# Transposing all of x beside the second stage of a convolution, and giving the dense slices to the third

## The chip, the cores and the metric

The kernel runs on one core of one Trainium2 chip. The metric is the time of one execution on the device in microseconds (us); lower is better. Six runs of the kernel before took 2141.81 to 2153.86 us, with a median of 2148.28.

## The reference

Two unrelated computations share one launch; their outputs stand side by side.

*A* is a long convolution over a sequence of 2048 rows and 1024 channels. A key is filtered with four taps, multiplied by a value, convolved along the sequence with a kernel `ssm_k` as long as the sequence, and multiplied by a query:

```python
y_f = rfft(kv_pad) * rfft(ssm_k_pad)
y = irfft(y_f)[:S] + kv * ssm_D
out_a = q * y
```

*B* is a recurrent attention over 64 segments of 32 rows. Each segment sees its own rows and an 8-row memory, and its output at the memory's rows is the memory of the next segment:

```python
for s in range(64):
    h = concat([mem, x[32*s:32*s+32]])
    q, k, v = h @ Wq, h @ Wk, h @ Wv          # 1024 -> 32 heads x 128
    o = softmax(mask(q @ k.T * scale)) @ v
    o = o @ Wo
    mem, out_b[s] = o[:8], o[8:]
```

All inputs and outputs are bf16.

## The kernel before, in words

**A in three stages.** The transforms are done as matrix products with sines (a transform of 4096 as 128 times 32). Stage 1 makes the first half of the transform of u (the product of filtered key and value) and of the convolution kernel, and stores both to scratch tensors in HBM, SU and SK. Stage 2 has 17 sets of frequencies, each in two halves of 512 channels: 34 *units*. A unit (`unit_front`, `unit_back`) takes the gathered tiles Kg and Ug, multiplies them by tables on TensorE (Kre, Kim, Ure, Uim into PSUM, line 323), copies Kre and Kim to SBUF on ScalarE (L335, L336), forms the complex product on VectorE (pa, pb, pc, pd, L343 to L346, and Yim, L350) and GpSimd (Yre, L349), and multiplies back into z on TensorE (L358, L360), which ScalarE copies to zs (L362) and stores to the scratch SZ (L301). The matmuls of a unit fill half of TensorE's columns (L323) or of its rows (L358, L360), and two of them run side by side. Stage 3 has 16 rows of work: each loads a tile zt from SZ (L389) and every second one a tile qt (L396), both on SyncE's queue; TensorE makes y from zt with four matmuls (L392), VectorE multiplies it by qt into ot (L399), and GpSimd's queue stores ot for two rows at once (L401).

**B's preparation beside it.** Before the recurrence starts, the parts of B that do not depend on the memory are computed by plain dense products, for the memory-sized part of each segment. XBT, the transposed rows of x that the dense products use, is made between stages 1 and 2. `dense` (from L608) is a generator that gives one *slice* at a time: eight matmuls of 128x512 (L614) into a PSUM tile kb_ps, then a copy to a tile `stage` by `evac` (two of three on ScalarE, L603, one on VectorE, L605). Sixteen slices make one group. The first group (K, first half) runs between stages 1 and 2. Three more groups, 48 slices, are given by `slices`: K's second half, Q's first half, Q's second half. When a group is finished, its result is stored to a scratch tensor REC in four stores (L643), one for each later call of `fill`. The weights of these groups lie in tiles Wmid and pw. Two of the pw tiles for Q's second half (pw 2 and 3) can be loaded (L567) only when the group before, which uses the tiles, is through.

The recurrence also needs all of x transposed, not only the memory-sized part. `x_block(b)` (from L584) takes one of 16 blocks of 128 rows: eight TensorE transposes (L591) from X_sb into a PSUM tile xt_ps, one copy to xt (L593), one 256 KB store to REC on GpSimd's queue (L594). X_sb is one buffer that holds two blocks; `x_load` (L580) loads it on SyncE's queue, right after the second block of the pair before has been transposed. xt is one buffer for two blocks as well, so the first copy of a pair waits until both stores of the pair before have landed. xt_ps and kb_ps share a pool of two PSUM buffers.

**What sets the order.** `fill` is called after each of the 34 units of stage 2 and after each of the 16 rows of stage 3; n counts the calls, 0 to 49. In the kernel before, n with n % 3 == 2 gives a block of x, so that 11 blocks (n = 2, 5, ..., 32) lie in stage 2 and 5 in stage 3. Every other unit of stage 2 gives one dense slice (23), and every row of stage 3 gives one slice as well (16). Nine slices are left and follow stage 3; then comes the projection V (L749), 256 matmuls of the same size, for which the weights Wres and Wmore are loaded (L563, L567) into memory that stage 3 held until its last y. At odd n above 5 a weight tile is copied to the scratch WS (L669), from n = 29 on six chunks of Wo are copied to WS (L663). A scheduler then orders the instructions of each engine by its own estimates of their times: it moves the matmuls of a slice between those of neighbouring units, and some past the end of a stage. Each engine and each DMA queue then works through its own list in that fixed order.

**The recurrence.** 64 steps of attention with weights streamed from WS (L709); its order is written out by hand, and the change does not touch it.

Of the kernel before, what the change touches and what calls it, by code (L numbers as in the profile page):

```python
# [405 lines left out]
def b_kernel(ctx: ExitStack, tc, x, mem0, Wq, Wk, Wv, Wo, outb, n_seg, run_a):  # L406
    nc = tc.nc
# [35 lines left out]
    def dram_chunk(ch):  # L443
        m, a, g = ch
        return Wo_v[a] if m == 3 else W_v[m][a, g]

    def dst_view(ap, ch):
        return ap.rearrange("p (hh d) -> p hh d", hh=2) if ch[0] == 3 else ap

    def stream_src(ch):  # L450
        return WS[ring_order.index(ch), :, 0:2048]
# [123 lines left out]
    copies = []  # L575
    loaded = {}

    def x_load(b):
        t = base.tile([128, 2048], BF, tag="wring2", name="X_sb")
        x_loads.append(nc.sync.dma_start(t[:].rearrange("p (b d) -> p b d", b=2),  # L580
                                         x[b * 128:(b + 2) * 128, :].rearrange("(b p) d -> p b d", b=2)))
        loaded[b], loaded[b + 1] = t[:, 0:1024], t[:, 1024:2048]

    def x_block(b):  # L584
        X_sb = loaded.pop(b)
        if b % 2 == 0:
            t = base.tile([128, 2048], BF, tag="wring3", name="xt")
            xts[b], xts[b + 1] = t[:, 0:1024], t[:, 1024:2048]
        tp = ps0.tile([128, 1024], BF, tag="ps0", name="xt_ps")
        for kc in range(8):  # L590
            nc.tensor.transpose(tp[:, kc * 128:(kc + 1) * 128], X_sb[:, kc * 128:(kc + 1) * 128], ident[:])  # L591
        xt = xts.pop(b).rearrange("p (s k t) -> p s k t", s=4, k=8)
        nc.vector.tensor_copy(xt, tp[:].rearrange("p (k j t) -> p j k t", k=8, j=4))  # L593
        rec_stores.append(nc.gpsimd.dma_start(REC[:, 4 * b:4 * b + 4, 0:256], xt.rearrange("p s k t -> p s (k t)")))  # L594

    xts = {}
# [44 lines left out]
    def store():  # L641
        if stores:
            nc.gpsimd.dma_start(*stores.pop(0))  # L643

    units = [0]
    blocks = list(range(n_seg // 4))
    wo_copies = [ch for ch in ring_order if ch[0] == 3]

    def q1_load(kc, k, ins):
        res[1, kc, 1] = pw(k)[:]  # L650
        with tc.issue_after(ins):
            group(1, 1, which=[kc], ws=q1, held=True)

    def fill(behind=None):
        store()
        n = units[0]
        units[0] += 1
        if n == 0:
            x_load(0)
        if n >= WO_COPY and wo_copies:  # L660
            ch = wo_copies.pop(0)
            with tc.issue_after(rec_stores[-1].ins):
                nc.gpsimd.dma_start(dst_view(stream_src(ch), ch), dram_chunk(ch))  # L663
        if n in Q_LOAD:
            i = Q_LOAD.index(n)
            q1_load(kept_q1[i][1], 4 + i, behind.ins)
        if n > 5 and n % 2 and copies:
            with tc.issue_after(rec_stores[-1].ins):
                copied.append(nc.gpsimd.dma_start(*copies.pop(0)))  # L669
        if n % 3 == 2 and blocks:  # L670
            b = blocks.pop(0)
            x_block(b)
            if b % 2 and blocks:
                x_load(b + 1)
        if n >= 34 or n % 3 != 2:
            next(rest, None)

    run_a(ps0, pw, slot16, stage1_done, fill)

    wres3 = ctx.enter_context(tc.tile_pool(name="b_wres", bufs=1, reuse_waits="tile"))  # L680
# [173 lines left out]
    with tc.manual_schedule():  # L854
# [53 lines left out]
        for s in range(n_seg):  # L908
            b, j = s // NB, s % NB
# [256 lines left out]
```

## Time and profile before

| | us |
|---|---|
| median of six runs | 2148.28 |
| the profiled execution, its own time | 2148.14 |
| span of its records, from first to last instruction | 2145.6 |
| stage 2, first to last matmul | 144.0 to 276.4 |
| first y of stage 3 to start of the last | 286.0 to 337.8 |
| dense slices left over | 338.6 to 355.5 |
| V projection | 355.5 to 411.8 |
| recurrence | 411.8 to 2145.6 |

How to read the profile: a table by windows gives, for each stretch of time, the microseconds for which each engine was busy and in brackets how many instructions it ran; then the TensorE clock that was granted as a share of full speed, the mean busy share of the 16 DMA engines, and what they moved. PE is the TensorE matmul, PEld its weight load, DVE is VectorE, ACT ScalarE, POOL GpSimd, SP SyncE. Matmuls overlap each other in the records, so the distance between their starts says more than their duration. A timeline row gives the start, the duration, the engine, the line, what is written and what it is made from, and in square brackets how long the engine was idle before it and what ended that. A name with a q behind it (SPq) is the engine's own queue of commands. A row of a group ends with total busy time and mean nanoseconds of one instruction, and after the second bar the idle time before them and what ended it.

Over the whole span TensorE is busy for 81%, the DMA engines move 374 GB/s on average, and the granted clock is 0.982.

### The profile page before, as it was taken

How to read it: one execution, taken by the hardware profiler on the slowest of the kernel's cores; microseconds unless marked ns; L12 is line 12 of the kernel's file. 1: busy time of each engine (PE TensorE's matmuls, PEld its weight loads, DVE VectorE, ACT ScalarE, POOL GpSimd, SP SyncE). 2: the span in 40 equal slices, each digit the busy share in tenths (PEclk: the TensorE clock that was granted, in tenths of full speed). 3: DMA queues.
4: the chain of work that ended last, by engine and by line, in shares of the span. 5: the costliest groups of instructions: out<-in, count | busy, mean ns of one | idle time of the engine just before them, and what ended most of it. 6: DMA issues, size and time to landing. Idle time of an engine off the chain costs nothing. (4 is left out here: it accounts for less than half of the span.)

```text
span 2145.6 us, 81545 instructions
## 1 busy us (share of the span) xinstructions
PE 1743.6 (81%) x35732; PEld 944.1 (44%) x35764; DVE 866.2 (40%) x2735; ACT 638.2 (30%) x1131; POOL 431.6 (20%) x1108
## 2 busy tenths in 40 slices
PE   6889879888888888788778877878877878887886
PEld 2433334344444444444444444444444444444444
DVE  9828842133333333333333333333333333333332
ACT  6946511222222222222222222222222222222221
POOL 3114522211111111111111111111111111111111
PEclk9999999999999999999999999999999999999999
DMA  8989899999999999999999999999999999999996
GB/s 306 364 322 355 297 342 381 309 396 385 382 388 393 390 392 391 390 387 392 382 385 393 393 389 379 391 390 384 374 385 378 390 388 389 393 396 390 377 383 268
DMA packets 238313, 802.29 MB, mean 374 GB/s; under 512 B 34722, under 2 KB 34754, under 8 KB 237956
## 3 DMA queue, kind: packets, MB, share of 16 engines
q1 hardware_dynamic: 206036, 724.01, 87.9%
q0 software_dynamic: 26704, 62.59, 8.5%
q10 hardware_dynamic: 5216, 10.49, 1.3%
q8 instruction: 279, 4.57, 0.9%
q14 instruction: 78, 0.64, 0.1%
HBM read 737.56 MB, written 62.39 MB: 373 GB/s over the span
## 5 line engine op out<-in xcount | busy, mean ns | idle before, releaser
L942 PEld LDWEIGHTS <-rec 128*32 128x32 bf16 x12351 | 322.7, 96 | 463.8 <-issue 239.6
L942 PE MATMUL acc<-wring,rec 128*32 128x512 bf16 x3765 | 377.6, 385 | 128.6 <-DMA wring<-WS 113.2
L951 ACT CAST qkv_sb<-acc 128x512 bf16<-128x512 f32 x384 | 225.1, 586 | 648.9 <-PE acc L942 646.0
L1028 PEld LDWEIGHTS <-OT 128*32 128x32 bf16 x8192 | 222.0, 98 | 182.0 <-issue 154.2
L1028 PE MATMUL yacc<-wring,OT 128*32 128x256 bf16 x3072 | 156.0, 280 | 98.0 <-DMA wring<-WS 62.1
L942 PE MATMUL acc<-Wmid,rec 128*32 128x512 bf16 x3072 | 227.1, 384 | 0.0
L942 PE MATMUL acc<-Wres,rec 128*32 128x512 bf16 x2816 | 221.6, 380 | 0.0
L888 PEld LDWEIGHTS <-OTB 128*16 128x16 bf16 x4096 | 105.4, 89 | 101.6 <-issue 93.0
L1014 ACT CAST OT<-OTp 128x512 bf16<-128x512 f32 x128 | 75.0, 586 | 243.6 <-PE OTp L1006 243.4
L1044 DVE COPY KT<-tps 128x512 bf16<-128x512 bf16 x64 | 27.2, 425 | 292.8 <-PE tps L957 292.8
L1015 DVE CAST OTB<-OTp 128x128 bf16<-128x128 f32 x128 | 37.4, 292 | 263.0 <-ACT OT L1014 263.0
L843 POOL DMA_DIRECT2D rec<-REC x64 | 37.5, 586 | 518.7 <-issue 264.0
L787 DVE TENSOR_SCALAR wring<-OTp 128x384 int32<-128x384 int32 x126 | 112.3, 891 | 53.5 <-PE acc L942 45.6
L942 PE MATMUL acc<-pw,rec 128*32 128x512 bf16 x1544 | 132.1, 385 | 0.0
L918 POOL COPY KT<-rec 128x128 bf16<-128x128 bf16 x128 | 38.9, 304 | 418.5 <-PE SB L966 410.7
L903 POOL DMA_DIRECT2D out_dram<-YB x128 | 73.3, 579 | 242.8 <-DVE YB L901 222.6
L972 DVE TENSOR_REDUCE mx<-SB 128x5 f32<-128x200 f32 x128 | 47.1, 368 | 177.1 <-PE SB L966 177.0
L888 PE MATMUL SB<-wring,OTB 128*16 128x256 bf16 x1488 | 78.7, 275 | 39.4 <-DVE SB L867 30.7
L957 PEld LDWEIGHTS <-qkv_sb 128*128 128x128 bf16 x1024 | 62.9, 97 | 105.7 <-ACT qkv_sb L951 68.4
L957 PE MATMUL tps<-ident,qkv_sb 128*128 128x128 bf16 x1024 | 101.4, 222 | 8.0 <-DVE wring L787 0.2
L1028 PE MATMUL yacc<-Wlate,OT 128*32 128x256 bf16 x2048 | 105.5, 276 | 1.3 <-ACT qkv_sb L951 0.7
L1084 ACT CAST Y<-yacc 128x256 bf16<-128x256 f32 x64 | 23.8, 373 | 249.7 <-PE yacc L1028 245.7
(233 smaller groups left out, 2692.7 us busy)
## 6 DMA issues: line engine op xcount, KB each, us to landing
wring<-WS SPq DMA_DIRECT2D x1215, 512.0 KB, 7.4
rec<-REC POOLq DMA_DIRECT2D x64, 192.0 KB, 6.1
SK<-s_sb SPq DMA_DIRECT2D x16, 512.0 KB, 7.0
SU<-s_sb SPq DMA_DIRECT2D x16, 512.0 KB, 8.2
Kg<-SK SPq DMA_DIRECT2D x32, 256.0 KB, 5.1
Ug<-SU SPq DMA_DIRECT2D x32, 256.0 KB, 6.6
REC<-stage POOLq DMA_DIRECT2D x16, 512.0 KB, 10.7
zt<-SZ SPq DMA_DIRECT2D x16, 512.0 KB, 8.2
```

The lines of the kernel that those rows point to most:

```text
L787: nc.vector.tensor_scalar(out=dst, in0=src, scalar1=0, scalar2=None, op0=ALU.bitwise_or)
L843: nc.gpsimd.dma_start(rec[:], REC[:, s, :])
L888: nc.tensor.matmul(self.acc[32 * dq:32 * dq + W, x - o:y - o], lhsT=self.OTB[:, c, 4 * g + i, :], rhs=r, start=first and not self.seeded, ...
L903: nc.gpsimd.dma_start(bass.AP(outb.tensor, outb.offset + (SEG * NB * self.b + NX) * 2048 + 256 * dq, [[2048 * SEG, NB], [2048, 8], [1, 256 ...
L918: nc.gpsimd.tensor_copy(KT[:, :, :, 32:40], KBs[:, 128 * g:128 * g + 128].rearrange("p (c i t) -> p i c t", c=4, i=4))
L942: nc.tensor.matmul(self.acc[32 * c:32 * c + 32, x - 512 * c:y - 512 * c], lhsT=hT[:, kc, :], rhs=r, start=(kc == 0 and x == 512 * c), stop ...
L951: nc.scalar.copy(sb[:], self.acc[:])
L957: nc.tensor.transpose(tp[:, i * 128:(i + 1) * 128], sb[:, i * 128:(i + 1) * 128], ident[:])
L972: nc.vector.tensor_reduce(out=mx[:], in_=S, op=ALU.max, axis=AX.X)
L1014: nc.scalar.copy(OT[:], o_view[:, :, :, 0:32])
L1015: nc.vector.tensor_copy(OTB[:, :, 4 * g:4 * g + 4, 8 * j:8 * j + 8], o_view[:, :, :, 32:40])
L1028: nc.tensor.matmul(yacc[32 * dq:32 * dq + 32, x - o:y - o], lhsT=OT[:, c, i, :], rhs=r, start=(h == 0 and x == o), stop=(h == 31), tile_po ...
```

## The change

All of x is transposed beside stage 2: a block at every odd n, so that blocks 0 to 15 come at n = 1, 3, ..., 31. The other units of stage 2 give one dense slice each (17). In stage 3 the calls give one slice at even n and two at odd n (24). By this count seven slices are left for after stage 3. The copy from xt_ps to xt moves from VectorE to ScalarE. The copies of weight tiles to WS move from odd to even n. Buffers, loads and stores are the same.

```diff
         xt = xts.pop(b).rearrange("p (s k t) -> p s k t", s=4, k=8)
-        nc.vector.tensor_copy(xt, tp[:].rearrange("p (k j t) -> p j k t", k=8, j=4))
+        nc.scalar.copy(xt, tp[:].rearrange("p (k j t) -> p j k t", k=8, j=4))
         rec_stores.append(nc.gpsimd.dma_start(REC[:, 4 * b:4 * b + 4, 0:256], xt.rearrange("p s k t -> p s (k t)")))
...
-        if n > 5 and n % 2 and copies:
+        if n > 5 and n % 2 == 0 and copies:
             with tc.issue_after(rec_stores[-1].ins):
                 copied.append(nc.gpsimd.dma_start(*copies.pop(0)))
-        if n % 3 == 2 and blocks:
+        if n % 2 and blocks:
             b = blocks.pop(0)
             x_block(b)
             if b % 2 and blocks:
                 x_load(b + 1)
-        if n >= 34 or n % 3 != 2:
+        for _ in range(1 + n % 2 if n >= 34 else 1 - n % 2):
             next(rest, None)
```

## The prediction

> **What bounds the kernel now.** I read the page's time slices first, then a table of windows by stage, then the timelines of TensorE, VectorE, SyncE and GpSimd over those windows, and last the waits of each line that the change touches.
>
> ```profile
> core 0: us, PE busy (x) PEld busy (x) DVE busy (x) ACT busy (x) POOL busy (x), PEclk, DMA share, GB/s
> 144.00:276.40 132.40, 122.51 (x676) 41.66 (x686) 108.36 (x190) 78.79 (x150) 66.92 (x67) 1.00 0.93 323
> 276.40:286.00 9.60, 6.66 (x35) 2.98 (x36) 1.72 (x3) 1.76 (x3) 1.58 (x2) 1.00 0.79 283
> 286.00:338.60 52.60, 39.07 (x171) 16.61 (x174) 22.56 (x22) 4.10 (x7) 13.11 (x16) 0.94 1.02 391
> 338.60:355.50 16.90, 16.79 (x78) 7.64 (x79) 4.26 (x8) 3.52 (x6) 1.84 (x3) 1.00 0.92 338
> 355.50:411.80 56.30, 55.10 (x252) 25.03 (x256) 6.92 (x10) 12.89 (x22) 17.64 (x21) 1.00 0.94 328
> 411.80:2145.60 1733.80, 1389.57 (x33985) 796.12 (x33983) 624.41 (x2244) 441.30 (x833) 304.16 (x958) 0.98 1.00 384
> ```
>
> The rows are stage 2, the gap to stage 3, stage 3, the dense slices left over, the V projection, and the recurrence. The change touches only the first four; the last two keep their instructions, so I carry 56.3 and 1733.8 us over unchanged. Stage 2 is TensorE's (122.5 of 132.4 us busy, and little of the rest is queued elsewhere); stage 3 is held by transfers (DMA share 1.02, TensorE 39 of 52.6); the dense rest and V are TensorE's again.
>
> Inside stage 2 the pace follows from the order of the built instructions on TensorE. From the timeline: a dense or y matmul takes a slot of 0.216 us, a pair of 64-row or 64-column ones 0.216 for both, a transpose 0.056, and each change between these shapes adds 0.11 (a lone pair starts 0.32 after the last). Counted so, the 70 us from unit 5 to unit 24 come out 3.6% short, so I scale counts by 1.036. Two stalls stand out of it:
>
> ```profile
> 230.88 0.23 PE L591 MATMUL xt_ps<-ident,X_sb 128*128 128x128 bf16 x1
> 231.14 0.38 SPq L580 DMA_DIRECT2D X_sb<-in_B_x_dram  x1
> ...
> 239.29 0.45 PEld L591 LDWEIGHTS <-X_sb 128*128 128x128 bf16 x8 [0.23 <-DMA X_sb<-in_B_x_dram]
> ...
> 245.42 0.69 DVE L593 COPY xt<-xt_ps 128x1024 bf16<-128x1024 bf16 x1 [6.50 <-DMA REC<-xt]
> ```
>
> X_sb is one buffer for two row blocks: the next load goes out 0.3 us after the second block's last transpose and here lands 8.1 us later, just when TensorE comes back, three units on. And the copy to xt, also one buffer per pair, waited 6.5 us on VectorE for the pair before to be stored. From unit 24's first matmul to unit 27's took 16.4 us where the count gives 11.3: that wait costs TensorE 5.1 us.
>
> **The change, part by part.**
>
> *Dense slices and blocks in stage 2.* By the code, stage 2 gets 17 slices in place of 23 and 16 blocks in place of 11. The built order says less: up to the last z matmul TensorE has 165 dense matmuls (194 before), 128 transposes (96) and 291 changes of shape (263). So -29 x 0.216 = -6.3, +32 x 0.056 = +1.8, +28 x 0.11 = +3.1: only -1.4 us. Of this, unit 4 must be left out: its Kg lands no earlier, at 158.9 us. From there the count is 107.3 before and 105.1 after: **-2.2 us**.
>
> *Moved transfers.* Each block brings half a 512 KB load on SP and a 256 KB store on POOL. Stage 2 moved 42.7 MB; four more blocks bring 2 MB, while K's stage stores (four of 512 KB) move from units 23-26 to its last units. 323 GB/s stands against 391 in stage 3, so I cost bandwidth at nothing; if that cover is missing, 2 MB at 391 GB/s cost 5 us. On SP, the next sets' gathers stand behind X_sb's issue, but a set is fetched some four units (14 us) ahead and lands within 5 to 7: nothing; without that lead each pair would lose about 1 us. On POOL four more store issues of 0.78 us, and the copies to WS at even instead of odd units, stand ahead of Yre; POOL is busy for 67 of 132 us and waits 49 us for pb: nothing, uncovered 3 us.
>
> *The X_sb load.* This is the wait that the change adds. Between a pair's last transpose and the next pair's first, TensorE now has, counted and scaled, 3.9, 5.6, 6.3, 6.3, 5.7, 6.3 and 6.3 us (before: 8 to 11). It needs 0.3 + landing. Landings of these loads in stage 2 were 6.5 to 8.1 us, median 7.2. So waits of 2.7 (the first gap holds unit 4's wait too), 1.9, 1.2, 1.2, 1.8, 1.2, 1.2: **+11.2 us**, all on TensorE, with z and the next unit's matmuls queued behind. Ends: at 5.6 us (the shortest landing) 1.6, at 8.1 us 17.5. The Trainium skill, "DMA: Bandwidth & Descriptors", Measured, gives 0.95 us for 64 KB and 6.15 for 1 MB, leaving out descriptor emission; between them 512 KB is an estimated 3.3 us, under every gap, and the waits would be 0. The row has the other queues' traffic in it, so I take the row.
>
> *The store wait.* The 5.1 us go, for the place of that collision goes: K's stage stores no longer lie between blocks 7 and 8. Also about **1** us of today's X_sb waits (weight loads, 1.6 us in three). But ScalarE now waits where VectorE did, with Kre, Kim and zs queued behind it. A store is issued some 1.35 us after its copy starts and landed after 4.9 to 10.1 us, median 6.4 in stage 2. With the X_sb wait the next pair's copy follows 8.3 to 10.1 us after: enough up to 6.9 us of landing. Ends: 0, and 7 x 1.3 = 9 us at 8.2, a stage-3 landing. Near the median: **+1**.
>
> *The copy on ScalarE.*
>
> ```profile
> L249 ACT COPY kt<-k_tp 128x1024 bf16<-128x1024 bf16 x16 | 16.4, 1053 | 3.4 <-PE k_tp L247 3.4
> L593 DVE COPY xt<-xt_ps 128x1024 bf16<-128x1024 bf16 x16 | 10.9, 683 | 14.6 <-DMA REC<-xt 14.4 <-PE xt_ps L591 0.2
> ```
>
> The first row is a ScalarE copy of the same size and memories: 1.05 us for VectorE's 0.68. ScalarE's two units hold four Kre/Kim at 0.48, four zs at 0.53, two thirds of a dense copy (0.4) and two store issues (0.82): 5.3 us, with xt 6.3. TensorE needs 7.0 for two units. Cost nothing; uncovered it would be 16 x 1.05 = 17 us. The Trainium skill, "ScalarE: Activation LUTs", Rules for kernel authors, speaks against it: simple work belongs on VectorE, up to 3x faster. At 3 x 0.68 = 2.05 us ScalarE would need 7.3 us and set the pace, +4 us in all. The row says 1.5x, so I keep nothing. VectorE's freed 0.68 per block gains nothing either: it had 18% slack.
>
> Stage 2: -2.2 - 5.1 - 1 + 11.2 + 1 = **+3.9 us**, ending near 280.
>
> *Stage 3.* The gap stays 9.6 us: it is the last SZ store's landing and the first zt load.
>
> ```profile
> 312.24 0.38 PE L614 MATMUL kb_ps<-XBT,pw 128*128 128x512 bf16 x1 [4.52 <-DVE xt L593]
> 312.49 0.76 POOL L594 DMA_DIRECT2D REC<-xt  x1 [4.56 <-DMA pw<-in_B_Wq_dram]
> ...
> 337.77 1.02 PE L392 MATMUL y_ps<-zt,G2h 128*128 128x512 bf16 x4 [1.63 <-DMA zt<-SZ]
> ```
>
> The 4.5 us at 312 are put down to xt, but the weights pw of Q's second half landed there too (issued 303.3, 8.9 us). They can be loaded only once the second dense group is through, which in the new order is just before y10, not after y7. So y0 to y10 takes its ten zt steps of 2.5 us (TensorE has 22.0 of it), pw is issued 0.5 us later and lands after 8.9: 34.9 us. Behind the waiting matmul then stand y12 to y15 and 54 dense matmuls, 11.7 + 2.6 us to y15's start: 49.2 against 51.7 before: **-2.5**. The zt loads of y13 to y15 queue on SP behind pw, but have 8 us to spare at 8 us of landing, none at the 16.9 seen. Four blocks' stores and copies leave the stage; they were hidden or in the stall. Ends: -6 (1.5 MB at 391 GB/s less, and pw at 6.5) to +5.
>
> *The dense rest.* It has 72 matmuls for 78, -1.3 us. But V's eighth weight chunk landed 18.5 us after y15's start, and TensorE would want it at 0.9 + 15.6 + 1.5 = 17.9: 0.6 us of it turns into a wait: **-0.7**. The -3.5 us that two slices fewer would suggest is not there.
>
> Sum: +3.9 - 2.5 - 0.7 = +0.7 on the profiled execution's own 2148.14 us (span 2145.6 and 2.5 outside), which is the median of 2148.28 within 0.15: **2149 us**.
>
> **Rivals.** *Slower: stores too late for ScalarE.* Its place is the first xt copy of each pair; it decides from a store landing of 6.9 us. For it: VectorE waited 14.4 us there with three units of room, and now there are two. Against: most landings of stage 2 were below. At 8.2 us for stores and 8.1 for X_sb: +9 - 1 + 6.3 = +14, so 2163; with half of that, 2156.
> *Faster: X_sb comes in time.* If the last waits vanish (landing 5.6 us, seen in stage 3), 11.2 becomes 1.6: 2139. For it: TensorE's waits also thin out the traffic. Against: no landing in stage 2 was so short.
> *Slower in stage 3:* pw and zt landing late (16.9 us), +5 instead of -2.5: 2157; part of the slower case.
>
> **Numbers.** A measurement of this kernel can tell about 0.3%, 6.4 us, from no change. Forecast (within that) 0.44; faster 0.27, around 2139 to 2141; slower 0.29, around 2156. The range 2139 to 2160 leaves out about 2 in 10.
>
> **What would show it.** Right: xt transposes waiting 1 to 2 us for X_sb once per pair; stage 2's last z near 280; no VectorE wait for REC; a pw wait of some 8 us near y11; y15 near 339; V at 356. Wrong: ScalarE waits for REC of more than 5 us in sum, landings of X_sb below 6 us, or a stage 2 under 128 us.

## The result, and the profile after

The changed kernel took 2155.54 us (median of 34 runs, 2144.30 to 2168.03), the kernel before on the same chips 2148.08 (71 runs, 2139.36 to 2163.67): a ratio of 1.003, 95% interval 1.0019 to 1.0040, so 4 to 9 us slower. The forecast of 2149 is 6.5 us too low; the range holds the time.

The profiled execution of the changed kernel has a span of 2147.1 us, near the low end of its runs. Its recurrence took 1726.6 us where that of before took 1733.8, though its instructions are the same. So the comparison is made up to V's end, and over all kernels: the median less the end of V in the one profile lies between 1732 and 1740 us for before, after and the twelve experiments alike. By and large the differences between the medians come from the first 420 us; but the 8 us between these figures are as large as the loss itself, so a single profile shows where a time goes and not how large it is in the median. Windows by stage, in the columns used before:

```profile
core 0: us, PE busy (x) PEld busy (x) DVE busy (x) ACT busy (x) POOL busy (x), PEclk, DMA share, GB/s
142.80:285.30 142.50, 125.65 (x678) 43.96 (x689) 102.94 (x177) 91.46 (x163) 70.31 (x72) 0.95 0.88 306
285.30:296.40 11.10, 6.67 (x31) 2.83 (x30) 0.69 (x1) 2.34 (x4) 0.17 (x1) 0.94 1.02 342
296.40:347.00 50.60, 43.41 (x179) 17.98 (x183) 21.46 (x20) 5.86 (x10) 10.83 (x13) 0.95 0.95 348
347.00:362.50 15.50, 15.45 (x73) 7.02 (x73) 4.27 (x8) 2.93 (x5) 1.85 (x3) 1.00 1.01 354
362.50:420.50 58.00, 55.58 (x254) 25.12 (x258) 7.36 (x12) 12.89 (x22) 18.25 (x25) 1.00 0.93 340
```

Read against the rows of before: stage 2 grew from 132.4 to 142.5 us, the gap from 9.6 to 11.1, V from 56.3 to 58.0; stage 3 and the dense rest shrank by about 2 and 1.3. In stage 2 TensorE is busy for 3 us more and idle for 7 us more, and its granted clock is 0.95, not 1.00. Where in stage 2 this happens shows in the start of each unit's first product (pa, VectorE), counted from the first Kre matmul; the last three rows are experiments, told below:

| us from first Kre | unit 4 | unit 6 | unit 21 | unit 33 | last z |
|---|---|---|---|---|---|
| before | 17.4 | 24.9 | 79.1 | 128.4 | 132.4 |
| after | 18.3 | 32.9 | 90.2 | 137.2 | 142.4 |
| first pair early | 18.7 | 27.3 | 84.4 | 130.1 | 135.8 |
| all halves, early, ScalarE | 19.1 | 28.5 | 87.6 | 133.0 | 138.7 |
| all halves, early, VectorE | 18.5 | 26.3 | 80.2 | 125.7 | 130.3 |

Seven of the ten microseconds are lost between units 4 and 6 (14.6 us against 7.5). From unit 6 to unit 33 the two kernels take the same (104.3 and 103.5), though before has its REC stall in there. At the loss, SyncE's queue and then TensorE in the changed kernel:

```profile
154.85 0.32 SPq L293 DMA_DIRECT2D Ug<-SU  x1
157.60 0.38 SPq L580 DMA_DIRECT2D X_sb<-in_B_x_dram  x1
158.35 0.79 SPq L293 DMA_DIRECT2D Kg<-SK  x1
```

```profile
153.77 0.62 PE L591 MATMUL xt_ps<-ident,X_sb 128*128 128x128 bf16 x8
...
160.47 0.64 PE L323 MATMUL Uim_ps<-Ug,Mim 128*64 128x512 bf16 x2
166.71 1.03 PE L591 MATMUL xt_ps<-ident,X_sb 128*128 128x128 bf16 x8 [5.60 <-DMA X_sb<-in_B_x_dram]
```

Block 1 is transposed by 154.4. The load of the next pair goes out at 157.60, not 0.3 us later: SyncE's queue waited 2.4 us before it, by the trace until a Ug gather had landed. It lands after 9.1 us, and TensorE has stood still for 5.6. Then the clock (rows of 3.41 us of the changed kernel, then two rows of 4 us of before):

```profile
155.19:158.60 3.41, 1.38 (x8) 0.50 (x5) 0.42 (x1) 1.09 (x3) 0.04 (x1) 1.00 1.05 389
158.60:162.01 3.41, 2.51 (x8) 0.41 (x7) 3.38 (x7) 3.35 (x6) 1.93 (x2) 0.50 1.05 344
162.01:165.43 3.42, 0.00 (x0) 0.00 (x0) 1.96 (x4) 0.00 (x0) 1.14 (x1) 0.50 1.01 362
165.43:168.84 3.41, 2.13 (x14) 1.09 (x16) 0.00 (x0) 0.10 (x1) 0.00 (x0) 0.50 0.15 58
168.84:172.25 3.41, 3.08 (x11) 0.93 (x8) 1.30 (x3) 2.05 (x4) 0.00 (x0) 0.50 0.56 171
172.25:175.66 3.41, 3.41 (x17) 1.00 (x16) 1.60 (x3) 2.49 (x5) 1.36 (x2) 1.00 0.79 295
```

```profile
156.00:160.00 4.00, 2.44 (x14) 0.81 (x12) 1.07 (x2) 1.74 (x4) 1.64 (x2) 1.00 1.04 370
164.00:168.00 4.00, 3.73 (x19) 1.15 (x18) 3.41 (x7) 2.82 (x7) 2.48 (x4) 1.00 1.04 378
```

The first figure after the five busy times is the clock: 0.50 from 158.6 to 172.25. It fell before the wait for X_sb began (161.1): TensorE had just stood for 2.0 us before unit 4's Kre, by the trace for the copy of the Kre before it, which ScalarE started only when a Kg gather had landed. So the wait for X_sb did not bring the clock down; it kept it down. From 166.7 to 172.3 TensorE works at half speed (starts 0.43 us apart, not 0.216), which costs an estimated 2.8 us, half of this stretch, beside the wait.

The end of stage 2 (TensorE's timeline, after):

```profile
280.57 0.38 PE L360 MATMUL z_ps<-Yim,Nim 64*128 64x512 bf16 x1
...
285.01 0.39 PE L358 MATMUL z_ps<-Yre,Nre 64*128 64x512 bf16 x1
285.23 0.38 PE L360 MATMUL z_ps<-Yim,Nim 64*128 64x512 bf16 x1
...
296.45 1.01 PE L392 MATMUL y_ps<-zt,G2h 128*128 128x512 bf16 x2 [4.48 <-DMA zt<-SZ]
```

The last z stands behind 4.1 us of dense matmuls in TensorE's fixed order, and y0 comes 11.2 us after it.

### The profile page after: what moved, and what is told of

Read it like the earlier page. It is cut to its first block, busy times and chain, and to the rows that moved or that the text cites. A ratio compares the mean times of both kernels' runs of the same rounds, so it can differ in the third digit from the quotient of the medians.

```text
span 2147.1 us, 81561 instructions
## 1 busy us (share of the span) xinstructions
PE 1743.4 (81%) x35732; PEld 940.6 (44%) x35764; DVE 858.3 (40%) x2719; ACT 652.8 (30%) x1147; POOL 431.4 (20%) x1108
## 5 line engine op out<-in xcount | busy, mean ns | idle before, releaser
L1028 PEld LDWEIGHTS <-OT 128*32 128x32 bf16 x8192 | 217.1, 96 | 176.9 <-issue 149.6
## 6 DMA issues: line engine op xcount, KB each, us to landing
REC<-stage POOLq DMA_DIRECT2D x16, 512.0 KB, 10.1
```

The source lines that it names most:

```text
L1028: nc.tensor.matmul(yacc[32 * dq:32 * dq + 32, x - o:y - o], lhsT=OT[:, c, i, :], rhs=r, start=(h == 0 and x == o), stop=(h == 31), tile_po ...
```

## The experiments

All were measured with the kernel before beside them; the table gives the profiled parts in us (from the first Kre matmul to the last z, to y0, to y15, to V, to V's end, and their sum). Each profile is one execution, and the part sums follow the ratios only by and large.

| kernel | stage 2 | gap | stage 3 | rest | V | sum | ratio to before, 95% |
|---|---|---|---|---|---|---|---|
| before | 132.4 | 9.7 | 51.7 | 17.7 | 56.5 | 268.0 | |
| after | 142.4 | 11.2 | 49.6 | 16.4 | 58.2 | 277.9 | 1.0030 (1.0019 to 1.0040) |
| after, copies on VectorE | 137.7 | 13.4 | 53.3 | 16.4 | 56.9 | 277.6 | 1.0066 (1.0043 to 1.0090) |
| before, copies on ScalarE | 140.5 | 7.2 | 54.4 | 19.4 | 57.0 | 278.5 | 1.0030 (1.0017 to 1.0043) |
| before, stage 3 changed | 133.8 | 10.4 | 54.6 | 11.2 | 71.9 | 281.9 | 1.0064 (1.0040 to 1.0087) |
| after, first pair early | 135.8 | 10.8 | 50.8 | 16.4 | 57.7 | 271.5 | 1.0012 (0.9998 to 1.0026) |
| after, half loads | 138.7 | 11.3 | 48.6 | 16.4 | 59.3 | 274.2 | 1.0007 (0.9991 to 1.0023) |
| after, z first | 139.5 | 14.1 | 54.8 | 16.4 | 56.3 | 281.2 | 1.0048 (1.0033 to 1.0063) |
| after, stage 3 undone | 144.1 | 11.1 | 44.8 | 32.5 | 55.4 | 288.0 | 1.0070 (1.0047 to 1.0093) |
| early, VectorE | 137.4 | 14.3 | 52.9 | 16.4 | 58.1 | 279.1 | 1.0039 (1.0024 to 1.0054) |
| before, all halves | 137.3 | 9.4 | 53.2 | 17.7 | 57.0 | 274.6 | 1.0021 (1.0003 to 1.0038) |
| all halves, early | 138.7 | 10.7 | 51.9 | 16.4 | 58.2 | 275.9 | 1.0004 (0.9988 to 1.0020) |
| all halves, early, VectorE | 130.3 | 13.6 | 53.7 | 16.4 | 57.7 | 271.8 | 1.0015 (0.9999 to 1.0031) |
| the same, K's stores held | 131.3 | 9.8 | 54.3 | 16.4 | 57.3 | 269.1 | 1.0012 (0.9999 to 1.0025) |

**The copies back on VectorE.**

```diff
-        nc.scalar.copy(xt, tp[:].rearrange("p (k j t) -> p j k t", k=8, j=4))
+        nc.vector.tensor_copy(xt, tp[:].rearrange("p (k j t) -> p j k t", k=8, j=4))
```

> The changed kernel with the xt copies back on VectorE, nothing else. Theory A (the lost time is TensorE's wait for X_sb at the second pair and the half clock behind it): the same as the changed kernel, 2153 to 2158 us, and the 5.6 us X_sb wait near 161 to 167 us of the profile stays. Theory B (the ScalarE copy stands ahead of Kre and Kim, and VectorE's products, Yre and z come late by it): VectorE's waits for Kre fall from 25.7 us to about 5, and the time falls by 4 to 8 us, to 2148 to 2151.

2160.2 us: neither theory, 3.6 in a thousand slower than after. VectorE's waits for Kre do fall (us in total, times, longest; after first, then here):

```profile
DVE pa L343 <- ACT Kre L335: 25.7, 16, 6.9
```

```profile
DVE pa L343 <- ACT Kre L335: 5.1, 3, 2.1
```

In the profile stage 2 is 4.8 us shorter, with a wait of 6.2 us for X_sb in it, and the gap and stage 3 are 5.8 us longer: what stage 2 gains here is given back behind it. The profiled execution took 2151.65 us and was the fastest of its nine; why the median is slower than after's, the profile does not show. The built order explains stage 2: up to the last z it has 241 changes of shape and 158 dense matmuls, after has 291 and 165, which at 0.11 and 0.216 us is 7.0 us less to do.

**The copies on ScalarE alone, on the kernel before.**

```diff
-        nc.vector.tensor_copy(xt, tp[:].rearrange("p (k j t) -> p j k t", k=8, j=4))
+        nc.scalar.copy(xt, tp[:].rearrange("p (k j t) -> p j k t", k=8, j=4))
```

> The kernel before with only the xt copies moved to ScalarE. Theory A and the prediction's term (a copy on ScalarE costs nothing): 2145 to 2150 us, no change against before. Theory B: 11 copies in stage 2 at the same price give two thirds of the loss, 2152 to 2155, with VectorE's waits for Kre above 15 us (4.8 before).

2156.2 us, 0.30% slower, and waits for Kre of 20.7 us: what theory B expected, 1 us above its range. Stage 2 is 8.1 us longer. Its order has 20 more dense matmuls and 11 more changes of shape before the last z (274 for 263), 5.5 us; the rest goes with a clock of 0.86 and 0.80 between 150 and 170 us. One line on another engine has reordered TensorE.

**Stage 3 alone, on the kernel before.**

```diff
-        if n >= 34 or n % 3 != 2:
+        for _ in range(1 + n % 2 if n >= 34 else n % 3 != 2):
             next(rest, None)
```

> The kernel before with only stage 3's slices changed: three for every two rows. The prediction's terms for stage 3 and the dense rest, taken for this kernel: -2.5 us there and less in the rest, 2144 to 2147 us. Rival C (the weights of Q's second half and the zt loads come late behind the denser work): 2150 to 2157.

2162.43 us, 0.64% slower, more than either side expected. Only one slice is left for the dense rest, and V starts 2.3 us earlier, before its weights (TensorE's waits in V):

```profile
PE vb_ps L749 <- DMA Wres<-in_B_Wv_dram: 11.6, 6, 4.7
PE vb_ps L749 <- DMA Wmore<-in_B_Wv_dram: 2.0, 2, 1.5
```

Rival C had a loss, but by other transfers. The part belongs to a kernel whose stage 2 gives fewer slices, as the later run with stage 3 undone shows.

**The first pair early.** Blocks 0 and 1 at units 0 and 1.

```diff
-        if n % 2 and blocks:
+        if (n == 0 or n % 2 and n != 3) and blocks:
             b = blocks.pop(0)
```

> The changed kernel with the first two row blocks at units 0 and 1 in place of 1 and 3, so that the second X_sb load goes out some 7 us earlier; the other blocks stay. Theory A: the X_sb wait of 5.6 us at the second pair and the half clock (0.50 from 160 to 172 us) go, and the time falls by 4 to 8 us, to 2148 to 2151. Theory B: within 2 us of the changed kernel, 2154 to 2158.

2152.34 us, between the two ranges; the ratio goes from 1.0030 to 1.0012. Units 4 to 6 take 8.6 us, not 14.6, and TensorE waits 1.2 us for X_sb in all. The clock still falls, with hardly a wait for X_sb, but for 6.8 us in place of 13.7:

```profile
159.19:162.60 3.41, 2.58 (x12) 0.91 (x12) 2.99 (x5) 3.41 (x8) 1.15 (x1) 0.50 1.05 370
162.60:166.02 3.42, 3.32 (x12) 0.74 (x12) 3.30 (x6) 1.85 (x3) 2.33 (x3) 0.50 1.03 343
166.02:169.43 3.41, 3.19 (x15) 0.96 (x15) 2.26 (x4) 2.23 (x5) 0.93 (x2) 1.00 1.04 403
```

Taken whole, the edit gives back 6.3 of the 9.8 us in the profiles and, with intervals that still overlap, about half of the loss in the medians. Not all of it is the wait of theory A: the built order has 21 fewer changes of shape up to the last z (270 for 291) and one dense matmul less, 2.5 us by count, most of it behind unit 6.

**Half loads.** X_sb is one tile whose halves are loaded in turn.

```diff
-        t = base.tile([128, 2048], BF, tag="wring2", name="X_sb")
-        x_loads.append(nc.sync.dma_start(t[:].rearrange("p (b d) -> p b d", b=2), ...
+        if not xsb:
+            xsb.append(base.tile([128, 2048], BF, tag="wring2", name="X_sb"))
+        loaded[b] = xsb[0][:, 1024 * (b % 2):1024 * (b % 2) + 1024]
+        x_loads.append(nc.sync.dma_start(loaded[b], x[b * 128:(b + 1) * 128, :]))
...
-            if b % 2 and blocks:
-                x_load(b + 1)
+            if len(blocks) > 1:
+                x_load(b + 2)
```

> The changed kernel with X_sb loaded in halves: one 256 KB load per row block, each sent when the block two before has been transposed, so that a load has four units in place of two. TensorE's order stays the same. Theory A (the X_sb wait and the half clock behind it are the loss): no wait for X_sb is left, 2148 to 2151 us; if waits at the later pairs count too, it lies below the kernel with the first pair early (2152.3). Theory B (the order of instructions and ScalarE's queue are the loss): 2153 to 2157.

2152.93 us, at the edge between the two; the ratio, 1.0007, is lower than after's, with a slight overlap of the intervals. TensorE waits for X_sb no more at all, and with the order of after units 4 to 6 take 10.1 us, not 14.6: this is the cleaner test of theory A, and stage 2 is 3.8 us shorter. Units 6 to 33 take 106.2 us against 104.3 with the waits, but here a half clock from 168.6 to 175.4 reaches into them and costs up to 2.4 us, so the later waits may still have been worth their 1 us or so.

**The last z first.**

```diff
+                last_z[:] = [nc.tensor.matmul(pt[:, :], lhsT=Nim[rs, st, :], ...
...
+        if n >= 34:
+            with tc.issue_after(last_z[0].ins):
+                for _ in range(1 + n % 2):
+                    next(rest, None)
```

> The changed kernel with stage 3's dense slices held behind stage 2's last z matmul in TensorE's order. 29 dense matmuls (6.3 us at 0.216) that stood ahead of it go behind it. Theory C (the last z, its store and so the first zt loads are late by these slices): y0 is 3 to 5 us earlier and the time 2150 to 2153 us. Rival: the slices only change places, and the transfers or the slices themselves hold y0 and stage 3: within 1.5 us of the changed kernel, 2154 to 2157.

2160.76 us: a ratio of 1.0048 for after's 1.0030, with intervals that overlap, and above both ranges. Theory C falls. TensorE's timeline:

```profile
282.22 0.63 PE L361 MATMUL z_ps<-Yim,Nim 64*128 64x512 bf16 x1
...
296.35 1.86 PE L393 MATMUL y_ps<-zt,G2h 128*128 128x512 bf16 x4 [5.67 <-DMA zt<-SZ]
```

The last z is 3 us earlier and y0 where it was: the first zt loads went out at 289.5 (291.3 in after) and landed after 6.9 us instead of 5.1. TensorE had its slices done at 290.7 and waited; its clock was 0.66 from 280 to 290 and 0.72 in the next 10 us. Stage 3 took 5.2 us more.

**Stage 3 undone in the changed kernel.**

```diff
-        for _ in range(1 + n % 2 if n >= 34 else 1 - n % 2):
+        if n >= 34 or n % 2 == 0:
             next(rest, None)
```

> The changed kernel with one slice per row in stage 3 again. Eight slices (64 matmuls, 13.8 us) go from stage 3 to the dense rest. The prediction's terms for stage 3 and the rest (three for two gains 3 us): 2157 to 2162 us. Rival, from stage 3 alone on the kernel before, which lost 13 us because V came before its weights: undone gains, 2143 to 2152.

2166.62 us, 0.70% slower than before and above both ranges. Stage 3, rest and V take 132.8 us against 124.2 in after: here the denser stage 3 gains 8.6 us, which the ratios bear out (1.0070 and 1.0030). V takes 55.4 us, with its weights in time. The rival falls for this kernel: what cost 13 us on the kernel before pays on the changed one, whose seven leftover slices (16.4 us) still cover V's weights.

**First pair early, copies on VectorE.** The first and the fourth edit together.

> The kernel with the first pair early (2152.3 us) with the xt copies back on VectorE. Theory B (with the copy on ScalarE the built order has 35 more changes of shape on TensorE, 270 for 235, and the products wait for Kre): 3 to 6 us faster, 2146 to 2149. Rival, after the first run with the copies on VectorE (4.7 us slower than the changed kernel): the waits for the REC store come back to VectorE, 2154 to 2158.

2158.27 us, where the rival had it: theory B falls again, now without the 5.6 us wait in the way. Stage 2 is no shorter than with ScalarE's copies (137.4 and 135.8): TensorE, ahead of them, waits 7.5 us for X_sb and VectorE 4.7 for the REC store. The gap is 3.5 us longer.

**All halves on the kernel before.** The halves of X_sb as above, and the same for xt.

```diff
-        if b % 2 == 0:
-            t = base.tile([128, 2048], BF, tag="wring3", name="xt")
-            xts[b], xts[b + 1] = t[:, 0:1024], t[:, 1024:2048]
+        if b == 0:
+            xts[0] = base.tile([128, 2048], BF, tag="wring3", name="xt")
```

> The kernel before with X_sb and xt each kept as one tile whose two halves are reused in turn: a load or a copy now waits for the block two before, not for the whole pair before. TensorE's order is the one of before. If the stall at units 24 to 27 is the pair's store (6.5 us of VectorE's wait, 5.1 us of TensorE's), it goes, and with it some 1 us of X_sb waits: 4 to 6 us faster than before, 2143 to 2146 us. Rival (the stall is GpSimd's queue with K's stage stores, and only its name was the store): within 2 us of before, 2147 to 2151.

2152.98 us, 0.21% slower; a miss for both. The REC wait and its stall are gone, and three units on stands a new one. SyncE's queue, then ScalarE with its queue, then TensorE:

```profile
238.73 0.97 SPq L293 DMA_DIRECT2D Ug<-SU  x1
```

```profile
251.30 2.92 ACTq L301 DMA_DIRECT2D SZ<-zs  x2
254.32 0.59 ACT L335 CAST Kre<-Kre_ps 128x512 bf16<-128x512 f32 x1 [5.92 <-DMA Ug<-SU]
```

```profile
249.93 0.39 PE L613 MATMUL kb_ps<-XBT,Wmid 128*128 128x512 bf16 x1
254.95 0.64 PE L323 MATMUL Kre_ps<-Kg,Mre 128*64 128x512 bf16 x2 [4.64 <-ACT Kre L335]
```

The Kg and Ug gathers issued from 233 to 245 landed after 11.9 to 15.1 us (median 6.0 over the stage), with K's four stage stores and two weight loads just issued. The Ug gather of 238.73 landed at 253.8. Until then ScalarE stood still: two stores of z are ahead of Kre in its queue, and the second of them and Kre started only when that gather had landed. TensorE's next unit waited 4.6 us for Kre, and TensorE then ran at half clock from 255 to 261. That the stall at units 24 to 27 of the kernel before is this burst of transfers, and the REC store only the first to be late in it, fits both profiles; a run without the burst at this place was not made on the kernel before.

**All halves and the first pair early, with each engine.** The edits above together on the changed kernel.

> The kernel with the first pair early (2152.3 us; TensorE's order stays the same) with halves for X_sb and xt as well, so that hardly a wait for either buffer can be left. If the buffers are what still separates it from before: 2145 to 2149 us. Rival (the loop from Kre over the products to Yre and z, with the copy in ScalarE's queue, sets the pace once the waits are gone, as in the kernel with half loads): 2151 to 2154.

> The same as the kernel with all halves and the first pair early, with the xt copies on VectorE. Against the kernel with the early first pair and VectorE's copies (2158.3 us) it loses the waits for X_sb (7.5 us) and for the REC store (4.7 us), some of which overlap: 2147 to 2151. If it comes out below the one with the copies on ScalarE, the copy's engine costs time by itself; if above, ScalarE's copy is a gain of its own.

2149.91 and 2150.99 us: not told apart from each other, nor from before. With hardly a wait for a buffer left, stage 2 takes 138.7 us with ScalarE's copies and 130.3 with VectorE's (270 and 234 changes of shape, 164 and 158 dense matmuls: 5.3 of the 8.4 us; ScalarE's also has a late gather and a clock of 0.66 between 200 and 210). The gap and stage 3 then take back 4.8.

**K's stage stores held.** On the last kernel; out_st holds stage 3's output stores.

```diff
-        if stores:
-            nc.gpsimd.dma_start(*stores.pop(0))
+        if stores and not 28 <= units[0] < 36:
+            with tc.issue_after(out_st[-1].ins) if out_st else ExitStack():
+                nc.gpsimd.dma_start(*stores.pop(0))
```

> The kernel with all halves, the first pair early and VectorE's copies (2151.0 us), with K's four stage stores of 512 KB held back from stage 2's end until the first output store of stage 3. TensorE's order stays the same up to the last z. If these stores are what lengthens the way from the last z to y0 (13.6 us there, 11.2 in the changed kernel, 9.4 to 10.4 where they lie some 40 us earlier): the way shrinks to 9 to 10.5 us and the time to 2146 to 2149, below every kernel tried, before among them. Rival (transfers only change places, and stage 3, which is held by them, gets the 2 MB back at 391 GB/s, 5 us): the way shrinks but stage 3 grows by 3 to 5 us, 2150 to 2152.

2152.61 us. The gap falls from 13.6 to 9.8 us, as theory and rival both expected, and stage 3 grows by 0.6, not by the rival's 3 to 5. TensorE's first y, without and with the hold (last z at 274.0 and 277.2):

```profile
287.65 1.87 PE L392 MATMUL y_ps<-zt,G2h 128*128 128x512 bf16 x4 [6.89 <-DMA zt<-SZ]
```

```profile
286.95 1.02 PE L393 MATMUL y_ps<-zt,G2h 128*128 128x512 bf16 x4 [3.05 <-DMA zt<-SZ]
```

So K's stores at stage 2's end lengthen the gap, by one profile of each. The sum to V's end is 2.7 us shorter, but the time expected did not come: the medians do not tell this kernel (1.0012) from the one without the hold (1.0015) or from before. No version beat the kernel before.

## Why the prediction was right or wrong, by its own steps

*The X_sb load, +11.2 us on TensorE.* The mechanism was right, the sizes were wrong in both directions, and the price of a slower clock behind a wait has no term in the prediction. Predicted were a wait of 2.7 us at the second pair and 1.2 to 1.9 at six later ones. At the second pair it was 5.6 us plus an estimated 2.8 of half-speed work. Two assumptions failed: "the load goes out 0.3 us after the last transpose" (3.2 us here, with SyncE's queue held up by a gather) and a landing of 7.2 us (9.1, at a DMA share of 1.01 to 1.05). Of later ones only one shows, 1.0 us at 199; the later landings were 4.5 to 8.0 us, the median of all eight 5.8. The prediction called landings under 6 us a sign that it was wrong, and they came. By the count and the waits, units 4 to 6 should have grown by about 1 us (2.7 of wait, 1.5 fewer to do), and grew by 7.1. That this is the largest part of the missing time is shown by two edits: the half loads, with TensorE's order kept, take 4.5 us back there, and the first pair early, with an order that is shorter as well, 6.0. Summed, 6.6 us of waits and 2.8 of slow work are 9.4 of the 11.2 us, near only by luck: one wait was far too small and six hardly came.

*The count, -2.2 us, and the REC stall, -5.1.* The count held between units 6 and 21 for the kernel before (54.2 us by count, 54.2 measured); after took 57.3 against 53.3. TensorE was busy for 52.7 us of that stretch in both kernels. The 3 us more are waits of the changed one, among them 1.6 for Yre, 1.0 for X_sb and 0.7 for the copy to xt. The stall of before did go; with the prediction's own scale of 1.036 on its count it was worth 4.7 us, not 5.1.

Behind it the table of pa misleads: from unit 25 to 33 the changed kernel took 32.4 us where before took 26.3, but before's VectorE was catching up there after its stall (busy for 24.0 of the 26.3). In the starts of TensorE's first Ure matmul, units 25 to 32 took 29.2 us in the changed kernel and 31.3 in before, where the counts are 25.6 and 25.8. Most of the 3.6 us over the count are TensorE's waits for Yre, 2.8 between 246 and 264; in all of stage 2 these are 4.4 us, 1.1 in before (us in total, times, longest; after, then before):

```profile
PE z_ps L358 <- POOL Yre L349: 4.4, 6, 1.3
```

```profile
PE z_ps L358 <- POOL Yre L349: 1.1, 3, 0.6
```

So the 3 us that the prediction named for an uncovered GpSimd, and put at nothing, are about what came. Its cover ("busy for 67 of 132 us") was an average over the stage. From 250 on, the last set's four clears of Kg and Ug (0.95 us each), of which the first waits 2.5 us for TensorE, and a REC store stand ahead of Yre in GpSimd's order. How much of the 4.4 us is this order is not shown: before's GpSimd was busier in the same stretch (9.5 of 10 us against 7.1), and with the copies on VectorE the waits for Yre are 2.0 us, so part of them may come with the products that ScalarE's copies make later.

*The copy on ScalarE, nothing.* In engine time this stands: 1.03 us each, and ScalarE's waits for the REC store were 3.7 us in three, under the mark of 5 and far from the slower rival's 9. Its price sat inside another term: with the copy on another engine the scheduler interleaves TensorE's matmuls differently, and the 291 changes of shape that the prediction counted would be 241 with VectorE's copies. On the kernel before the move alone costs 0.30%. In the changed kernel it is no loss, since the VectorE order pays the same later, in the gap and in stage 3: the ratios with the copy on ScalarE are the lower ones in all three pairs, by some 3 in a thousand in two of them.

*The gap, unchanged at 9.6.* It is 11.2, and 10.7 to 14.3 in every kernel that has K's stage stores at stage 2's end, but for the one that holds them back (9.8). The first zt load landed after 5.1 us, 3.5 in before. The prediction moved these stores and costed them only where they left, not where they went: by the last zs store.

*Stage 3, -2.5; the rest and V, -0.7.* From y0 to y15 it was 49.6 us, 49.2 predicted. The 8 us wait for pw near y11 did not appear (1.8 us); pw went out 28 us after y0, not 26, landed in 6.7 and 8.4, and the zt loads (5.0 us of waits after y0) had already held the rows back. The sum was right by luck, with another transfer in the role. (Its 34.9 us should have been 34.4: ten steps of 2.5, 0.5 and 8.9.) The rest gave 1.3 us, V lost 1.7.

In sum, +0.7 was predicted and +9.8 measured up to V's end in the profiles, +7.5 in the medians: of the 9.1 between, 6 are units 4 to 6 with the second pair, 1.5 the gap and 1.1 V, and the other errors inside stage 2 nearly cancel. The range holds the time, being 21 us wide. The slower rival's 2156 us is the time that came, but not by its mechanism: stores too late for ScalarE cost 3.7 us of waits in all.

What stays open: with every buffer wait removed and the first pair early, the profiled sum is 275.9 us, not below the kernel with the first pair early alone (271.5); a gather was late again near unit 16, and the clock at half for 6.8 us behind it. One profile each does not tell how often that falls so, nor how much of the half clock the other executions have. And the profiled execution of the changed kernel took 2148.86 us, 6.7 less than its median: the parts above are those of one of its shortest executions.

## What to carry to other kernels

When a single buffer is asked for more often, price its worst gap, not the median one: the time the load can be issued (what stands ahead of it in its queue), its landing at full DMA load, and the slow clock after the wait. A transfer that is moved away from one place has to be costed where it arrives, and a copy moved to another engine can be paid for in the order that a scheduler then gives a third. Removing the wait that the profile names may only let the next transfer of the same burst show itself.

## What the runs showed of the hardware

In the changed kernel the clock went to 0.50 after a stretch of 3.41 us in which TensorE was busy for 1.38 us and stood still for 2.0 in one piece. It stayed there for 13.65 us, four such stretches, and came back after the one from 168.84 to 172.25, the first in which TensorE was busy nearly throughout (3.08 us). With the first pair early it was at half for two of them. In the kernel before with all halves it fell after 2.3 and 0.6 us of work in two 4 us windows and came back 6.6 us after work resumed. In the kernel before, three windows of 4 us with 2.4 to 2.7 us each, from 240 to 252, kept 1.00. The Trainium skill ("TensorE: Matmul & The Clock Gate", Part 1) describes a gate with a free-running window of about 3.4 us, which goes to half after an idle window and back after a busy one. The half, the steps of 3.41 us and the way back agree with the rows; but the window before this fall was not idle, only 1.38 us full. A stall of TensorE thus can have a price beyond its length: an estimated 2.8 us on 5.6 here.

A DMA load of 512 KB took 4.5 to 9.1 us to land in one stage of one kernel, and the gathers of 256 KB 2.6 to 15.1 in another, by what was in flight. That spread, not the mean, decided what a single buffer cost.
